# The same kernel under another recorded order of its tasks: two transformer layers with recurrent memory on one core

## The chip, the cores and the metric

One core of a Trainium2 chip runs the whole program. The time is in device microseconds, from the first to the last instruction and what lies around them; the median of the runs counts. A profiled execution has a span of its own, which is a little shorter than its time.

## The reference

Four stages run one after another on x (2048 tokens of 512 numbers): memory attention, gated FFN, memory attention, gated FFN, each on the layernorm of x and added to x. The two attention stages use the same weights, and so do the two FFNs.

```
def _A_ref(x, mem0, Wq, Wk, Wv, Wo, seg_len):      # H = 32 heads of 128, M = 8, seg_len = 32
    mem = mem0
    for s in range(n_seg):                         # 64 segments
        xs = x[:, s * seg_len:(s + 1) * seg_len, :]
        h = jnp.concatenate([mem, xs], axis=1)     # 40 rows
        q, k, v = h @ Wq, h @ Wk, h @ Wv           # per head (einsum)
        p = softmax(where(mask, q @ k.T * scale, -1e9))
        o = (p @ v) @ Wo                           # summed over the heads
        mem = o[:, :M, :]
        outs.append(o[:, M:, :])
    return concatenate(outs)

def _B_ref(x, w_gate, w_up, w_down):               # F = 1792
    return (sigmoid(x @ w_gate) * (x @ w_up)) @ w_down

x = x + _A_ref(layernorm(x), ...); x = x + _B_ref(layernorm(x), ...)
x = x + _A_ref(layernorm(x), ...); x = x + _B_ref(layernorm(x), ...)
```

The memory makes the segments a chain: a segment's first 8 rows of output are the next segment's memory.

## The kernel before

The kernel runs the two attention stages interleaved. A step (`emit_step`, line 876) takes segment t of the first layer and segment t - 6 of the second one together, so that a product has 80 columns (40 rows of each); there are 70 steps, 58 of them with both layers. In a step the 32 heads go in groups of six (one of two): products for q and k of three heads (line 953), the scores (988), mask, softmax on DVE and ACT (1002 to 1019), a transpose of P by TensorE (1033, three heads together as 128 columns), a spreading of P (1040 to 1047), P times V (1062), and the product with Wo (1080), which adds up all heads in one PSUM bank. After four segments an FFN block runs (`ffn`, 1135), whose weights stream in through GpSimd's queue (POOL).

V is made apart from that. The x rows of V don't depend on the memory, so `v_pass` (732) makes them for 128 rows at a time in eight blocks of 512 columns (742): a block's PSUM bank is copied into a staging tile, and a transfer stores it in a scratch array in DRAM (`scr`). The steps load their rows from there (921). The memory rows of V are made within a step (`strips`, 867) and go by transfers from SBUF to SBUF (933). The start of the kernel makes many V passes beforehand, while the weights still land: passes with `boot` stage two blocks together in the tiles of the FFN weights (`bootp`), and their stores go through SP or POOL, whichever the planner finds free. `v_half` (769) makes half passes. Before any V product, x tiles are loaded (829, 844), normalised (`layernorm_T`, 682) and transposed by TensorE (702); `load_mem0` (664) transposes the first memory (675).

Nothing is issued in the order of the code. Every piece of work is a task that `Planner.add` (243) takes with its engines, its duration, what it reads and writes, and the buffers that it uses. `Planner.plan` gives every task a rank from a long recorded string (`SEQUENCE`, line 61: a permutation of the 13,975 tasks), and `forward` (305) plays through them with the recorded durations: an engine that is free takes the task with the best rank among those that are ready and whose buffers are free. What comes out is the order on each engine, which engine does a copy that ACT or DVE could do, and which buffer each task gets. `lat` is the time that the planner reckons from a task's end until its readers may run; a reader of a stored V block is planned by the store's `lat`.

`warm` (450) looks for planned gaps over 250 ns on TensorE, and `run` (1284) fills them with matmuls on a tile of zeros (line 1306) ahead of the task behind the gap. These are ordinary instructions of the program: 123 of them, 54,912 columns in all.

```
for k, q in enumerate(unpack(SEQUENCE, len(T))):
    T[q].tail = -float(k)
order = self.forward()
```

In the built program SP first issues two chunks of Wv, six tiles of x and two more chunks of Wv; mem0 comes as the fourteenth. TensorE begins with 36 fillers, a layernorm transpose, 5 fillers, a transpose, 2 fillers, a transpose, two V blocks and the transposes of mem0.

Of the kernel before, what the change touches and what calls it, by code (L numbers as in the profile page):

```python
# [20 lines left out]
P = 128  # L21
MEM = 8
SEG = 32
L = MEM + SEG
# [12 lines left out]
def mm_ns(n):  # L37
    return max(n / 2.4 + 2.5, 25.0)
# [23 lines left out]
;B756%3T07011TGtd}$tIX)_K?aoXMjK$e5vW-dZtal;JHk{mI&QgWrBP)D^s=qIMTulb6#Ttex8Kf#~kv<HpT50CBI-Wv_<q6M!((->U-jq&7OXGm^aKUz-b1T~IwfdQy+_5vgcj*=+W!DBzdRHorO{Dd_S?ytV  # L62
X@7rCk^wxcAc)4=C`W%eB7ph_RA0xEwgUD}Il2H4j=NEEulF>SC>v4tcBxTgs^XsEp||WMAxE4XG}4z4h{P#HriIz5@sgq3p(``|;%O{6n9DN&9w@GGf?b)4gqABL7Mqk9J4weWwCX<#g8gt;=n4fzFl?OT7b2wp
p}=YmBVMk|m_ezF7HBVJgMCuiBDemSwzRvJ(+BJu^W`JnXdoZ|kmZn9#z_o#s~WV33xdfAt9G|T8V*OhQyX?Uz;x;->E>P1`f}sQk0-3NRRf{h8>N0+jEl$!))6nCL~2Gjwoh~l+c&{=ux~QXxRU8QLzHm)5V&UF
^BvX>gX?a!Y+aN6KL))kLfWZTB1>|NA3M1R*p)P#*obLmB4jW&8Lm}UnO(pg7yocsBrUHD1T`khRq{_oAuirMSfMfwg5-3DA&drFdO&*lK7|~j`q8Q9ehoO8+=RbpwJDGrkF><F+@9DxSxxkyL>Wg@z}vmg#|dcp
9h_y&7uDJixd;LTL%N>RG6IlV2at9doK%w7qqU#N-lom3D7jt%<n%j_ahIsI`zmF^QFN;ha)U&K-$Yf}k;D!O$?X3(8|wh%qwho@H<1i*``u5MYCS`_6XF2MEposi3H$mI7Djl$;{}FG0(O_|w}0usw!t-Q$Kx<c
YQ^$YZzlxQyA0&1XYIlO^|;Fi#L0Bq+CTGPI?Yl!dvj*CT}^+8M71Oep{!lmu@=}*YS%MvO!JppJoS4W;go^Sjm(3>RkqLCftth|_jd+ATMRX8qG!&_MNFEkfn$<Qh|oFR_YiL*@n1RS-Z!?iym$42_~Q3?U?M5Z
1|m@WYnrc(_(Tg@%3T(QT{3~u=C55b<J#XbY+sm9j5QT~s<@CJ4w2~7%Cy{)LY2(Ns$d+|=X-=^UIMYMw;%5qRrPUu>D-N&&oremdbeLUkiOQmDU4!3U)jxu=ee7U|6T3h1Y2#$^vvd(XNnfMLH#@FT{>BMD3q+1
13cJ{`AIV>6SWna>`{uSOqvUqNRB|5^kKTOu&Bj3U!-kabDd_CuNb=+m{Ha6IpeJR-cQX}Fok{JYBOhh+ND)dX*NE$u$Xxfn&ZQH=4CFY60MTs2@CjsIt4K%E5mQJM4$+Vv^iETZ(^toahRM-+%3zew`Vfy+xXcC
=B^YXWBj)RD|K&dT7u?~SuD0_QYeR8WfrkQPti6k!~=ekT_7x%&Rk=rl=3A^TC9dQgt<5Nqk{B4pDlG$r-C140<!iYq10n!l9^U%5VDWv(9Q6L^oEOew8I1DGVCO+9ijD7|6vfRe-rN>%4AahcsE>(VZoH$D_aiq  # L70
UdFEj2nhiX^~=pCqMCq(R+c&$>o=;=$u`h_0Wq0x{O<70OOQjN6Se6q064$r%qo|uw12gCQsC?1umzgIKYL#~-ooQU03i+8;TBBM3Ncb_7A%0Q@9pb8>`8p8#J)b4<Yo{s2wHj&fFF0>>s?eU@c!=z;IhJN><MY4
dm_q}5+t3d3zqz9!Vhk$Ey}C(bE0K<^m%dn;dqb>etDy8CuW4qDBZ3Qp+iF+1!wkhP#lWcIl;^(XfM&iym)!wuZ{TVkM(A?u{3N4tM~ZeY*clT?9&f4ZZ&Xm<4yRlK;`WPYI}}MWb^<;uqs-kx>c7@tkMh2^jNA1
i1K(7xyZ8N0!9h47ikR6@5g%0H=s74#SYl(o56>%^M-`e<XohImgJWHnaW=t7W@3Cq81oc?!@=gzAW24{{lOh#F-;3bV0MadMuG-83~<sd6+pNE>~k^TmD3&2t3%rx$l&<d(|41?&z87MH{U&07s6K)O?4}Go5{G
#cP1w05yW3-A|q3OGSd*Jr4<|+^`@5B?AgT%^YS2((mAe-9#3ya}xI~9*6v*t`3Gr+q{<Y(*0H*FJY!Fh3Bur38a7#5wOBdW+Aa9v<J=-3F};Hw5F#ay$IqA5?yrf6Yy_^m;_ba4lK>HUO*`VKAVIdvj6`rcyQ)(
J2aQeC**Z(pkHlUO5-XB`(pPJx_mQz&l-Qov(Z>#H*!&DYAHr)GG}4N0nG-mK-2B>MHIapk%U*n;3*WyB!fMNwR~zpLtD~X*H)KviKe@lRenrbzNc{<+Y#TpDkr?=B+i)90ozo;du~g|hc#rkL6I}yHvPnI=ef){
GjOx#bmBXj=rMKD>BUrXXi=rs9sYFj(WrJDEQ$)B<d~cp;6fD#ZTXSh{&r}QvBMTAQ!nXfpEF!qV9f+7@^!R`nYFoPe{64^8IY$UWoR>`6zg`(`8wu{(Mj^4sKQC4`u^p}1pf*d4;QKuGN|3%{uG~8XA@C#GK#TK
|MNCI$Rg?<y(g)5Iug<AChsqZWL&40hy84US%XF#P0O;+Y`I!A`&mi?PO-(~lPQZCd7Y<XM1gnB+91a}{iwf2Aq6QHsb)izB0Y}byOIV_!K2AY$nxjPw&z;p<u(m;Lag})0Lys17bQ4+Z1BlLY{uWx#h6}?s-8<v
isqPSpfY2MMgoBY`$Hd@`4dP5langGki~+qs0b|DiNAH^K(tyZ=N62Fd|i28RYODmVvV<2>?_E!lt`1bnk&(PxZ7p!p4P{CC$QQbTMZ~B!f6Ej%-mk<4a6}Ak4fe(X`DT6bFY-=-bPQx&R(A8o~h&wW=LAbDzx^C
*2S67IF&Ex8QuX4pa+6UO!`LA<-<j!1rQpC;)rrT>$d!}7m_y3zt?FN8B%@Op{)0P#V_c>c{rb6%Cc+KrkE~gJ426|C3rbyIs!y5KtzN#vu69BA^}6YOWJpIK~%*ilp=L8Ym4PxY;`d+7jGm`L#6o=C|kSRKxp+s
12q#}B9C0lT4PZr!!3Mi|BK<#3Nl~x!ub0u)V+mlINC)@&%B1k$0I1Z?v_7yNRmlxHq*e;Q%iT0+g{R#-6#$Li$s^h>~P@Ffx!Q`k+(nl(nyRxP1ll##izuCdVkgGU)QEW0w}pC-@k2ZpCLRWdZ$qo<eDLb9cDAP  # L80
3!qGZ#lcymlMU|F^0|ggOc`jev<hWTv_H+z%%y(3ezrAC)Cluy>pG>W-KKLeSzi84VHi$HR}dvnIAi-Yfxw=PFk9D#|Cn$%G?Lli=o!)35`VY%J2g~@qDFmrujR6*;k0-+K=>_7EXj=*13#G-Tno(3GRj@ZFf;E^
)MStRA1kyWf*z})0Q0GUnI*R)Re)aFhdRd=!6=o@TI3WnAPptA0y5<OXt_f;*qeOn`bCD=^B&nq|Nq@8+N>aO{Y-r=GjKi)z0(rlj+5$**8LycFjN}GbvSf4nboGRr*oM@KFd=XGave-nt+lQNU7XUxQ9;9JD?GT
K`IsG<=4^#j7{mwd3$P?ux_W`Nq5ZTv_k#Oyw@$8n@%$H{Qt)hbFY0UK62=LerA~X;x!wGWy>D5iVc*wgWCsTt#xx{O&aJh^%=WUW~Y$a0;!^AdOJ3C8MN}6G#=}fUwJ6Il-%gMmR6LGSeUz?Y`EN^Oa@Q;uE+Ie
Kbkh(Y{p>W5BTj^oSqWg{K0)2P<9@mb*T3lD7b4zj%e9zi!*Bbpn0gIA685bppYu;m9-)*Cc^1JXyjw@`*|*36VGc5`^eA~OLXT(oR)K3A&(Z>IJ$jih7p&CubfDeaS1vSk*Ez~ZH9ODh6{h*-CMq!Sv6%HiMko+
<2Jyw<0zq<rwD@wL*ZR5S37mG)xF`SV6;uBVyQ`Ax@MFofhBVm0%%V{gDbs#ZRa!<Exes`29q)JlbJ!kM}TPHAkD#`RDAR#Ss3LFjq7yRe*{{X{-3OFa+?FXQ1H7%lqNLzGmRBlyz$kn+7C%<jtG7Fm<)g@|1iDq
^q)*nuQ`vDOg**bB&GFNqmk%Q8$})k13+Q>;sK`<=>-K?dm^NGb-voa_UoyY0e~Y&)D4@X^U&-d0y|RjqJE;X^FlS3wOst}_ntnQlfomib-*cLDnRvBkAoMid9*;k*ciCRD7U*ts*vgDHcWv~fABk<8=gu3fFT|b
{)DPOllg)4_;wu#R$vG$zs*#|9)$r4@-yXAHk)lqZ`#n4=&jo0Gs0OUi9x|PAyd|I)Y`OdcpcBW&yC5=y>|%1f3{4sgGAp+oE_kwTJ4BR=!AqA_Pfs-p7jUkIpV=%;J|bQtZ??SLWiZw6SI^O>fGH-gD6RT$pfqF
Z<6|is?Azbab$@G@7Ln=i8DaY{oTXAF*#7Qt6T~LtZ^u?EL9fQzPT|gl(WPkOCY2gKSs}Ved5z~TmQ?@pe_#IgZRr7hwG`cW6=WL(-Q?>2>JT$Y?banab$d!)xa7cTA)UPKc_h-?sku5!}SiS?D=rE&y$_`-s!EI
KC8IvcD?VGQ-4HSo75G({ZlxJmLZc7p|ySPq!(*u*-_VfrKaj(&T31}QD9~tF16O8a5w+4gkBkx<-nk}Y_IyVHo>Db2>w1{?)Q77h@rt=H>s@nC9#UDN#pfnZrQ--m22UtEj(~W!G8;QHsDuPB`6f?tod4oMo5-@
KRu<Olb)8-agn3Df#xtD(c2?D6J;1)Xy`&1`*ervi0*&eSYTQ!nk}JqG1jZ{axYS>fbe&C_h?=W?nawC<jUMwX_7Zy(r+=qlWm3@4Zw858T_wE=qLx$)-Jo&5p(po>fb7dNWy6xultjBq~p8*g`Qo1c{c_;_;1)S  # L90
n3jg-*HA?tG6PYwY}H<ZxF0s8hg{t&S)3;oaQ4@q90@RdTr?sO;udDHG$el4uW_VaDr)|06SOzvZ9$F%i&(x4`j1bT6sR%Z0Oi6ieMV;cmJc+7S|HE-t#XopGR={##V}&qWw9<`+(e#*u&VkWV>lIizR<cVO;q%5
ZS;Kg02(So7Cb;7z$FQdkfJ%}PiWuQuf0YvgJ5@aC`s<oqOZaDuhv)DNdVnI5e7)93ZTiHpHMwtx;A`y2x4WsiGXmP9d|!{_=vDfY|W4aUfcIgb_0V9+=jS!rtld92)*dy+IW=QADwfHSaA8MR!=2F(w$SpxGv#y
nFfjtw_;W{Tm;Rg05uhRMc=U!FlJaj=U%IAdbQW<zjSpi-WObAFDl{}l8?)2Y_d(k{u0#uQ$(vVn#eo{fo}AJQ?v;pvO^c8=<%qoj>)n#Mnm<i>8B2~X$xSi+v?C-vP2s3KS)a(NFudF<IMM(4kWhSTvtVDf*h}|
bTx>%ckueI?)M>$%OjuT{{VhIit*9My`gkr_0G<PJ%UJ6WhTpfyy1$`9Ox^+1?UOllYTZw@~Au|0=tYL?UB4`eK3}?Rs@vOv0||2B9*{QT1`Kk;jH$&(}+1|ua?cmu^8uMxL@oBqd1uhe#7XPx;f>NV)3W*xo*a`
s{EyzGY$f)ddVUJozvMCf*3?1je}$4w9%2Xu)B-XvAB&0rrD9O?T(DnSl@O#{%IHd?Wp5>EfwC8N$>PDNuz)Fc_^?(|KiH{^5n(rJ}Io4FgJ?Sv$)R3gmn_?syKoG8;*B#tX|@0tqD|QF4VuvAtAvDUezf32AHg+
a^`&DC6uG)WzKv%Ej|h(GEtd!dU#wS@$e-Uk^RX(a8-li<<6#<Jj<l4A1A;>)w{u`%wJMw^YmW<6>RULEZbMq^MQ|TmCuLO#?kZU)vs(!LS#s;n-WRbXm~d&kJG%?F7i83$OO5(lcIZeE-9b6a~?$yogjr#>1Xgr
GY>c3@wEx~WqJ#rO3kyONoAPvvm@dxg0FASj~Pl&vbkIM*FsI8E6>8@DRExc(%bKXyX+&g<(|YrEq7EP#UyX_h0XtHonqXe<o?Z?{7?!jx4U>a!oteG2*YZV@Z(*5f@;S1+rJa)4(Y3y%$PQEvDWWcDJDJth?IMP
vmP4c#NK$!{Hms>f=J8q^xxg+S-F<aTQz!BwzvJga@^2kG8T2?v~YINX{KUF(T%$$1z8yev=DrQcQ%N~QO%HXNmcHb3mMq=(SrlO%RT8DvOz4kznxN*%+^r)9fr;7WeZDrb1UOKKJrI)BIvExOo$81upoQ##Hzs0
Bg(5c0z&I{z7_!)0zSp0v1~1*?Wy%KjrNm*x|o3$>>v`WJm%?5$>7dIF9ge(yfqJ5eCA+xmo7p%nSZ;`v3+56PS~PL`4^0_?evmI4pJW3a>uhrcXkO#JpS;Oned_RPX#2u3>XmqMN4!Fo>?*P0_z(DHe=JEj0!5P
x`q!3mNPKGg7nD5_2ozUD$=lu95n}G<1B~f_0eR!of5_-SztT~CHCo6PJglym@xtJrYQ{m*m$QF4UI7AetPvO29CFM6#X{!RIAPvcHO{U%Ddb)Dj4M_*WQ4&Si%v|Ls>Sv5lz(*^wPP^5J?w8H?`Uwxdy6?pK+**  # L100
nOq)NIV0@!IqktP8R_T?=5v(}F|&!s0$n}&K7tfc)q~e=+H@Ye#xfR;yvd255@Sl*M5-GT0;;=0BNDuiIp&w8mjyK`VJ8Gv#C-uff<en&3aIj{c<YzXJS!GXvA^w0Q>ciR5Xr4DtQVxPnC(iDI^Z`7;BB3xZ(<6M
mck?rQ~R{xRu~ITyIi*IzJW$03lk{DL5HvEjN$7}J?|DvpK&H4WIn~IDoGG(CUjw_MAwtJCkHq)nFSfMnXzcSEX{ryU?Q%^J{{sg|2yolB;~oNt*rwUv$iv*?ZfTTBQ_m-3cb@&z$HNqPEdSorx4UbEQCg@W|IHj
^$JdW({`|Ix+}pZ<jp1M+joYWW8<H`5lZB<*#en<_hXoqHbXd#E0L$;YT)G1j5giiOn8!bTc_Hd%JF7G5E)GqXG<`%v)N}hJWumP?;Pd)#-fHhApq>|T)0TzF$D*gvo(M_d|f(si2qbFN63qfrTENy&_C%La!Z^e
A3GI4jhp#~G&Wr#*6j8sjxF?1$5w%8ga1(tcT>?hIoU;Bd&dF9d?IM)y~AtbV~7L(IA)w~;=O+4{|}F#qs=bRuky@$LMe!4&jn4WooMIlB^T;RgqOZgY7<m9>H2e9A^NN#r>{7^^3K%$4aBOp!XTw`>Jh33+X_=x
# [1281 lines left out]
```

## Time and profile before

| what | us |
|---|---|
| median of 3 runs | 1788.54 (1787.59 to 1789.13) |
| the profiled execution, its time | 1789.13 |
| its span | 1787.1 |
| TensorE busy | 1765.1 (99%) |
| ScalarE (ACT) busy | 1201.9 (67%) |
| VectorE (DVE) busy | 1184.6 (66%) |
| GpSimd (POOL) busy | 579.0 (32%) |
| products for q and k, line 953 (two groups) | 614.7 and 615.0 |
| products with Wo, line 1080 | 356.2 |

TensorE's instructions overlap one another, so that a group's mean of one times its count is more than its busy time. The fillers count as busy. By stretches of the span, TensorE is idle for 1.9 us between 300 and 400 us, for 0.2 to 1.3 us in each 100 us from 400 to 1700 us, and for 6.1 us in the last 38 us. DMA moves 153 GB/s on the mean and 345 to 391 GB/s between 10 and 50 us, while weights, x and the stores of V pass at the same time.

### The profile page before, as it was taken

The numbers are of one execution on the slowest core, as the hardware profiler recorded it, in microseconds if no ns is written. First come the engines' busy times: TensorE is split into PE (matmuls) and PEld (weight loads), VectorE is DVE, ScalarE is ACT, GpSimd is POOL, SyncE is SP. The second block draws the span as 40 slices with busy tenths as digits, with TensorE's granted clock in tenths as the row PEclk, the third lists the DMA queues.
The fourth block names the chain that finished last, engine by engine and source line by source line (L and its number), as shares of the span: only waits on it lengthen the run. The fifth ranks groups of instructions, "written<-read, shape, count | busy, mean of one in ns | idle before, by whom it ended". The sixth has DMA issues, their size and how long they took to land.

```text
span 1787.1 us, 91201 instructions
## 1 busy us (share of the span) xinstructions
PE 1765.1 (99%) x39305; PEld 1505.1 (84%) x39305; DVE 1184.6 (66%) x4075; ACT 1201.9 (67%) x3244; POOL 579.0 (32%) x837
## 2 busy tenths in 40 slices
PE   9999999999999999999999999999999999999998
PEld 4578788888888888988898898888888888989886
DVE  3477666676577667766676677667766765667675
ACT  5677777676666667666676677667666766666564
POOL 5414032522333242323334241333325232333432
PEclk9999999999999999999999999999999999999999
DMA  9835255634555464546546453556546454554543
GB/s 350 274 87 163 77 163 138 201 108 117 165 161 152 127 192 122 160 115 174 154 136 184 136 163 107 145 161 169 153 127 198 117 146 122 162 154 139 161 139 97
DMA packets 144766, 273.37 MB, mean 153 GB/s; under 512 B 34306, under 2 KB 82314, under 8 KB 144362
## 3 DMA queue, kind: packets, MB, share of 16 engines
q0 software_dynamic: 56704, 183.16, 35.2%
q1 hardware_dynamic: 87658, 84.38, 16.8%
q8 instruction: 308, 5.05, 1.2%
q14 instruction: 96, 0.79, 0.2%
HBM read 221.78 MB, written 27.07 MB: 139 GB/s over the span
## 4 chain that ended last, share of the span: by engine, by line
PE 90%; ACT 4%; DVE 3%; DMA 1%; issue 1%; SPq 1%; DVEq 0%; POOL 0%; ACTq 0%; POOLq 0%
PE bank L953 31%; PE bank L1080 16%; PE bank L1182 10%; PE bank L742 7%; PE bank L867 7%; PE bank L1205 5%; PE bank L988 4%; PE bank L1062 4%; PE bank L1033 2%; ACT pbt L1312 1%; PE bank L1306 1%; DVE st L1002 1%; PE bank L702 1%; ACT qku L1320 1%; PE bank L1150 1%
## 5 line engine op out<-in xcount | busy, mean ns | idle before, releaser
L953 PE MATMUL bank<-hT,wk_sb 128*128 128x80 bf16 (+3 forms) x8960 | 614.7, 198 | 1.1 <-issue 1.1
L953 PE MATMUL bank<-hT,wq_sb 128*128 128x80 bf16 (+3 forms) x8960 | 615.0, 198 | 0.7 <-issue 0.5
L1320 ACT CAST qku<-bank 128x480 bf16<-128x480 f32 (+4 forms) x770 | 379.7, 507 | 211.4 <-PE bank L953 173.4
L953 PEld LDWEIGHTS <-wq_sb 128*128 128x128 bf16 x8960 | 452.1, 99 | 23.9 <-issue 12.8
L953 PEld LDWEIGHTS <-wk_sb 128*128 128x128 bf16 x8960 | 446.9, 99 | 1.2 <-issue 1.2
L1002 DVE TENSOR_TENSOR st<-bank,cst 40x240 f32<-40x240 f32 (+3 forms) x768 | 278.6, 368 | 157.9 <-PE bank L988 147.2
L1080 PE MATMUL bank<-otsb,wo_sb 128*128 128x80 bf16 (+1 forms) x8960 | 356.2, 198 | 1.5 <-ACT otsb L1320 0.7
L1080 PEld LDWEIGHTS <-wo_sb 128*128 128x128 bf16 x8960 | 334.9, 99 | 15.5 <-issue 2.8
L1175 POOL DMA_DIRECT2D wu<-in_B_w_up_dram x217 | 164.0, 756 | 284.6 <-PE bank L1182 123.1
L1174 POOL DMA_DIRECT2D wg<-in_B_w_gate_dram x217 | 163.9, 756 | 263.1 <-PE bank L1182 138.7
L1320 ACT CAST otsb<-bank 128x480 bf16<-128x480 f32 (+3 forms) x420 | 198.1, 482 | 44.9 <-PE bank L1062 29.3
L1199 POOL DMA_DIRECT2D wd<-in_B_w_down_dram x217 | 153.7, 709 | 198.0 <-PE bank L1205 85.4
L1312 ACT ACTIVATE pbt<-bank,pbt 80x160 bf16<-80x160 bf16 (+4 forms) x488 | 181.6, 381 | 27.5 <-PE bank L1033 18.0
L1012 ACT ACTIVATE st<-st 80x240 f32<-80x240 f32 (+3 forms) x420 | 159.2, 382 | 31.0 <-DVE st L1009 28.4
L692 POOL TENSOR_TENSOR pbt<-pbt 128x1 f32<-128x1 f32 (+1 forms) x80 | 45.3, 568 | 391.3 <-DVE pbt L691 390.7
L1182 PE MATMUL bank<-xnT,wg 128*128 128x128 bf16 (+2 forms) x1784 | 171.5, 218 | 0.4 <-DVE st L1009 0.4
L1014 DVE TENSOR_REDUCE pbt<-st 80x6 f32<-80x240 f32 (+3 forms) x420 | 151.4, 363 | 29.9 <-ACT st L1012 27.3
L1182 PE MATMUL bank<-xnT,wu 128*128 128x128 bf16 (+2 forms) x1784 | 171.0, 218 | 0.0
L988 PE MATMUL bank<-qku 128*128 128x80 bf16 (+1 forms) x2240 | 163.1, 198 | 0.5 <-ACT qku L1320 0.2
L1009 DVE TENSOR_TENSOR st<-st,pbt 80x240 f32<-80x240 f32 (+3 forms) x420 | 154.5, 369 | 3.3
L1019 DVE TENSOR_TENSOR pbt<-st,pbt 80x240 bf16<-80x240 f32 (+3 forms) x420 | 153.8, 369 | 4.3
L1007 DVE TENSOR_REDUCE pbt<-st 80x6 f32<-80x240 f32 (+3 forms) x420 | 151.9, 363 | 4.2
(104 smaller groups left out, 2413.8 us busy)
## 6 DMA issues: line engine op xcount, KB each, us to landing
wg<-in_B_w_gate_dram POOLq DMA_DIRECT2D x220, 256.0 KB, 4.3
wu<-in_B_w_up_dram POOLq DMA_DIRECT2D x220, 256.0 KB, 4.3
wd<-in_B_w_down_dram POOLq DMA_DIRECT2D x220, 256.0 KB, 4.3
vsb<-scr SPq DMA_DIRECT2D x345, 48.0 KB
vsb<-sst SPq DMA_DIRECT2D x372, 32.0 KB
scr<-vst SPq DMA_DIRECT2D x112, 96.0 KB
vsb<-scr SPq DMA_DIRECT2D x230, 24.0 KB
wv_sb<-in_A_Wv_dram SPq DMA_DIRECT2D x8, 512.0 KB
```

The source lines that it names most:

```text
L953: nc.tensor.matmul(o_ap, lhsT=W[:, c, h * P:(h + 1) * P], rhs=mv(c), start=(c == 0), stop=(c == DC - 1))
L988: nc.tensor.matmul(s_all(SB)[:, w0 + i, :], lhsT=fview(qku[:, i, 0, 0:1], [(1, P)]), rhs=qku[:, i, 1, 0:ncol], start=True, stop=True)
L1002: pl.add("DVE", dve_ns(n, True), lambda gsz=gsz, hs=hs, st=st, SB=SB, pj_=pj_, npj_=npj_, mk=mk, idx=idx: nc.vector.tensor_tensor(out=st[p ...
L1009: pl.add("DVE", dve_ns(n), lambda gsz=gsz, hs=hs, st=st, mx=mx: nc.vector.tensor_tensor(out=st[pr, hs], in0=st[pr, hs], in1=mx[pr, hs].uns ...
L1012: pl.add("ACT", act_ns(n), lambda hs=hs, st=st: nc.scalar.activation(out=st[pr, hs], in_=st[pr, hs], func=ACTF.Exp, scale=self.scale), r=s ...
L1019: nc.vector.tensor_tensor(out=pb[pr, 0:gsz * L].rearrange("p (h k) -> p h k", k=L), in0=st[pr, hs], in1=rs[pr, 0:gsz].unsqueeze(2).to_broa ...
L1080: nc.tensor.matmul(WB[:, c * ncol:(c + 1) * ncol], lhsT=self.wo[:, h, c * P:(c + 1) * P], rhs=otsb[:, hl, 0:ncol], start=(h == 0 and c == ...
L1174: pl.add("POOL", 760, lambda wg=wg, fs=fs: nc.gpsimd.dma_start(out=wg[:], in_=self.wgv[:, :, fs]), r=[("wo", self.H - 1)], w=[gk] + bt, la ...
L1175: pl.add("POOL", 760, lambda wu=wu, fs=fs: nc.gpsimd.dma_start(out=wu[:], in_=self.wuv[:, :, fs]), r=[("wo", self.H - 1)], w=[uk] + bt, la ...
L1182: nc.tensor.matmul(gu[:, 2 * i + k, 0:n], lhsT=W[:, c, i * P:(i + 1) * P], rhs=xnT[:, c, rw], start=(c == 0), stop=(c == DC - 1))
L1312: nc.scalar.activation(out=dst, in_=src, func=ACTF.Copy, scale=by)
L1320: nc.scalar.copy(out=dst, in_=src)
```

## The change

Two things are edited. The recorded string is another one (147 lines of text instead of 108). And in the tasks of `v_pass` and `v_half` two details differ.

```
 SEQUENCE = r"""
...
 """
...
             if k % w == 0:
                 vs = pl.buf(self.bootp if boot else self.vstp)
             o = 512 * (k % w)
-            own = ("own", len(pl.bufs)) if k % w == 0 else own
-            pl.add("PE", DC * mm_ns(512), vmm, r=keys + [("wv", h) for h in range(4 * k, 4 * k + 4)] + [own] * (k % w), w=[B] + [own] * (k % w == 0), use=[vs])
+            pl.add("PE", DC * mm_ns(512), vmm, r=keys + [("wv", h) for h in range(4 * k, 4 * k + 4)], w=[B], use=[vs])
...
-                       lambda vs=vs, d=d, c0=c0, n=n: ("dma", d, vs[c0:c0 + BLK * n, 0:512 * w]), lat=3000.0 + 3000.0 * boot,
+                       lambda vs=vs, d=d, c0=c0, n=n: ("dma", d, vs[c0:c0 + BLK * n, 0:512 * w]), lat=3000.0 + 2000.0 * boot,
...
-                           lambda lo=lo, i=i, dd=dd, flat=flat: ("dma", dd, flat()[64 * i + lo:64 * i + lo + 32, :]), lat=3000.0 + 3000.0 * boot,
+                           lambda lo=lo, i=i, dd=dd, flat=flat: ("dma", dd, flat()[64 * i + lo:64 * i + lo + 32, :]), lat=3000.0 + 2000.0 * boot,
```

Without `own`, the two V blocks that share a staging tile in a `boot` pass may come in either order on TensorE; with it the first one came first. And the planner reckons 5000 ns instead of 6000 ns from the end of a `boot` store's issue until its readers may run. Both act on the order alone; no instruction's work depends on them.

The change was announced as "the P transposes of three heads take 128 columns of weights, 8 of them unused, instead of 120; P tiles and small columns share one tile; same order". The line that sets `m = P if w == 3 else w * L` (1030) and the tile `pbt` that holds P tiles and small columns (558) are in both kernels, so that the edits above are all.

What the other string makes of the order, by a comparison of the two built programs, task by task:

| engine | tasks | at another place | of these beyond the engine's first 115 | most places |
|---|---|---|---|---|
| TensorE | 4202 | 574 | 471 | 34 at the start, 21 later |
| ACT | 3243 | 2644 | 2542 | 38, 13 |
| DVE | 4073 | 3335 | 3236 | 21, 11 |
| POOL | 826 | 159 | 81 | 23, 7 |
| SP | 1631 | 793 | 704 | 29, 18 |

75 copies go from ACT to DVE and 74 the other way; six stores change between SP and POOL each way, and both programs have 7 `boot` stores on SP and 57 on POOL. TensorE's products are the same ones. The fillers are 129 with 57,984 columns.

At the start SP now issues two chunks of Wv, mem0, three heads of Wq (0.39 MB), four tiles of x, two chunks of Wv, and so on; the last two of Wv's eight chunks are behind 7.88 and 8.60 MB of issued transfers, with their own bytes, where they were behind 7.09 and 7.81 MB. Among SP's eight issues ahead of the second step's five loads of V (line 921) four are now stores of V, and a fifth stands between these loads, where there was one. TensorE begins with 18 fillers, the transposes of mem0, 26 fillers, and four layernorm transposes with 1, 2 and 2 fillers between them; then come V blocks.

## The prediction

> **What bounds the kernel now.** I read the page first: the busy shares and the chain that ended last.
>
> ```profile
> PE 1765.1 (99%) x39305; PEld 1505.1 (84%) x39305; DVE 1184.6 (66%) x4075; ACT 1201.9 (67%) x3244; POOL 579.0 (32%) x837
> PE 90%; ACT 4%; DVE 3%; DMA 1%; issue 1%; SPq 1%; DVEq 0%; POOL 0%; ACTq 0%; POOLq 0%
> ```
>
> TensorE (PE) is busy for 1765.1 of 1787.1 us and holds 90% of the chain. DVE and ACT stand idle for a third of the span, so moving their work costs something only where PE is made to wait. A change that leaves PE's products alone can move the time only through PE's idle time and through its filler: line 1306 issues matmuls on a zero tile whose results nobody reads, where the planner foresees a gap. I therefore looked next at the start of PE's order of time.
>
> ```profile
> 1.00 9.97 PE L1306 MATMUL bank<-otsb 128*128 128x512 bf16 x36 [1.00 <-DVE otsb L606]
> 10.81 0.39 PE L702 MATMUL bank<-cst,xn 128*128 128x128 bf16 x4
> 11.03 1.08 PE L1306 MATMUL bank<-otsb 128*128 128x512 bf16 x5
> 11.95 0.39 PE L702 MATMUL bank<-cst,xn 128*128 128x128 bf16 x4
> 12.17 0.43 PE L1306 MATMUL bank<-otsb 128*128 128x512 bf16 x2
> 12.45 0.39 PE L702 MATMUL bank<-cst,xn 128*128 128x128 bf16 x4
> 12.87 1.90 PE L742 MATMUL bank<-wv_sb,xvf 128*128 128x512 bf16 x8
> 14.70 0.25 PE L675 MATMUL bank<-cst,hff 8*128 8x8 bf16 x4
> 14.89 1.47 PE L742 MATMUL bank<-wv_sb,xvf 128*128 128x512 bf16 x6
> ...
> 17.70 1.02 PE L742 MATMUL bank<-wv_sb,xvf 128*128 128x512 bf16 x4 [0.69 <-DVE xvf L1322]
> ```
>
> Columns: start, us, instruction, and in brackets the idle time before it with what ended it. The first useful product is at 10.81; nearly all of PE's free time before that is filler and shows as busy. Then the same engine by stretches (busy us and count of each engine, granted clock, DMA share, GB/s):
>
> ```profile
> 0.00:10.00 10.00, 9.00 (x32) 3.70 (x33) 3.59 (x15) 1.28 (x1) 7.18 (x29) 1.00 0.84 272
> 10.00:20.00 10.00, 9.27 (x65) 4.87 (x64) 6.05 (x25) 4.91 (x13) 5.68 (x10) 1.00 1.09 345
> 20.00:30.00 10.00, 10.00 (x61) 4.60 (x59) 4.47 (x18) 7.42 (x18) 6.51 (x12) 1.00 1.08 379
> ```
>
> The DMA engines are full (share above 1) from 10 us on, so in the first 30 us a transfer lands by the bytes queued ahead of it. From 300 us on PE is busy for 98.1 to 99.8 us of each 100, so there is little left to win or to disturb there.
>
> **The change, part by part.** As built, both programs hold the same products, evictions and transfers. What differs is their order on each engine, and the filler: 123 matmuls with 54,912 columns before, 129 with 57,984 after, so +3,072 columns. The words about transposes with 128 columns instead of 120 describe nothing that changes: the line that sets m to 128 for a group of three heads, and the shared tile of P and small columns, stand in both.
>
> *Price of filler.* Five matmuls with 2,176 columns go from 11.03 to the next start at 11.95: 0.92 us, 0.423 ns a column. The first 36, with 18,176 columns, take 9.81 us (1.00 to 10.81) where this price gives 7.69; the 2.12 us on top are a slow first stretch. [...]
>
> *A, the first 15 us.* In the new order PE runs 18 fillers (9,088 columns), the four small transposes of mem0 (line 675), 26 fillers (13,312), and then four layernorm transposes with 1 + 2 + 2 fillers (1,792) between them, before the first V product. The 18 fillers end at about 1.00 + 2.12 + 9,088 x 0.423 = 6.96. The mem0 transfer is moved up to third place on SP, behind 1.05 MB of Wv; the first x tile before, behind 1.18 MB, is first read at 6.74 (the row of DVE below), so mem0 lands just before 6.96. Then 0.19 for mem0 (14.70 to 14.89), 26 fillers 5.63: first layernorm transpose at 12.78; four of them 0.88, fillers 0.76: first V product at 14.42. Before, PE has by 14.89 done three transposes, mem0 and two V blocks (12.87 to 14.70, 1.83); taking those V blocks off and adding the fourth transpose gives 13.28. The new start is 1.14 us behind. Against that stands the 1.0 us that PE loses before to waiting on the xvf copies (0.69 is in the rows above). If the new order waits as much, A is +1.14; if not at all, +0.1. I take the middle, +0.6.
> What hides the x tiles (DVE's first reading, and for C the second step's V loads on SP):
>
> ```profile
> 6.74 0.69 DVE L689 BATCH_NORM_STATS2 pbt<-xs 128x6 f32<-128x512 bf16 x1 [5.09 <-DMA xs<-in_A_x_dram]
> ```
>
> ```profile
> 81.43 1.91 SPq L921 DMA_DIRECT2D vsb<-scr  x5
> ```
>
> SP now issues 0.39 MB of Wq ahead of them. First tile: 1.58 MB instead of 1.18 MB, at 345 GB/s 1.2 us later, about 7.9; from first bn_stats to first transpose is 4.07 us (6.74 to 10.81), so 12.0, under 12.78. Fourth tile: 1.97 MB, 9.0, needed by 14.2 - 4.07 = 10.1. Both covered, by 0.8 and 1.1 us; beyond that each us is a us of PE.
>
> *B, the last chunks of Wv.* Before, the last is behind 7.81 MB of issued transfers, now 8.60 MB: with 2.72 MB in the first 10 us and 3.45 in the next, it lands at 20 + 2.43 / 0.379 = 26.4 instead of 24.3. PE reaches the product that needs it (twelve V blocks of 0.865, four transposes of 0.22, one half pass of 1.85 and two more V blocks after 14.42) at 29.3. Covered by 2.9 us: 0. At 345 GB/s and with the 2.5 us of the shortest boot store on top it would be 29.5, so at most +0.3.
>
> *C, the stores of V while the kernel starts.* The planner now reckons 5.0 us instead of 6.0 behind the issue (some 0.55 us). The row:
>
> ```profile
> DMA to landing us min/median/max: 2.5/5.3/7.1
> ```
>
> The median fits both, the longest neither. Four of these stores now stand on SP among the eight issues ahead of the second step's five V loads, and a fifth between them (one before). If SP waits there, those loads, an x load, a save of kx and the second step's strip loads (92.72 on before) are queued behind it, and PE's PV products wait for the strip loads without cover. But the V loads are issued at 81.43 to 83.3, over 9 us earlier: a landing of 7.1 costs nothing. The bound is one weight tile of 256 KB (0.7 us at 350 GB/s) pushed into the strip loads: 0 to +0.7, I take 0. [...]
>
> *D, the rest.* 471 of the 4,087 later PE stages change place, mostly by one; 149 copies change between ACT and DVE; 704 SP issues move. The filler there is 128 columns less (-0.05). PE's named waits on V loads are two, and the chain in order of time passes through a transfer four times:
>
> ```profile
> PE bank L1062 <- DMA vsb<-scr: 0.6, 1, 0.6
> PE bank L1062 <- DMA vsb<-sst: 0.4, 1, 0.4
> ```
>
> ```profile
> 218.98 3.06 DMA kx<-xq
> 312.58 4.17 DMA vsb<-sst
> 497.36 3.41 DMA vsb<-scr
> 1347.98 2.95 DMA vsb<-scr
> ```
>
> With 0.5 us a wait: four new ones +2.0, both old ones gone -1.0; I take +0.5. The last 38 us (31.93 busy) keep their order of products but for a few weights of the FFN: 0.
>
> Sum: 0.6 + 0 + 0 + 0.5 - 0.05 = +1.05 us on the profiled 1787.1, so a span of 1788.2. That execution took 1789.13; the median of the runs is 1788.54, so the forecast is 1789.6. Bounds: 0.1 - 1.0 - 0.05 = -0.95 and 1.14 + 0.3 + 0.7 + 2.0 - 0.05 = +4.1.
>
> **The rivals.** *Slower: the start's transfers set PE's pace.* If the queues share bandwidth among what is issued instead of serving in order, the two Wv chunks issued right behind the x tiles (1.05 MB) come with them: the fourth tile lands at 6.74 + (3.02 - 1.18) / 0.345 = 12.1, its transpose is at 16.1 instead of 14.2, and the filler has run out. +1.9 on A's 1.14, with C's 0.7 and D: +4.2, so 1792.7. It decides from a landing after 10.1. For it: DMA share 1.09. Against: by 6.74 some 1.6 MB can have moved before (2.72 MB of the first 10 us less 3.26 us at 345 GB/s) and 2.9 MB had been issued, so the first tile didn't share with all of it.
> *Faster side: the new start doesn't wait for xvf and D's two waits go.* -0.95: 1787.6. Against it: the gain is bounded by rows that add up to 2 us, and 1.3 us more filler is certain.
> *Nothing at all:* the words' transposes are unchanged, so the time is 1788.5; it speaks against this that the order did change.
>
> **How the numbers follow.** A measurement of this kernel can tell about 0.2%, 3.6 us, from no change: 1785.0 to 1792.1. Forecast (with the nothing case) 0.62, slower rival 0.27, faster side 0.11. Of the forecast 0.03 lies above 1792.1; of the slower rival 0.02 below; of the faster side 0.06 beyond -0.2%. So faster 0.06, same 0.66, slower 0.28. The range takes both bounds, the slower rival and a spread like that of the runs shown (0.8): 1787.0 to 1794.0.
>
> **What would show it.** The first V product at 14 to 15 us (right), after 16 (the slower rival); the product of the last Wv chunk without idle time before it; PE's wait on V loads at most 3 us in all; filler 129; the stretches from 300 us on as before within 0.5 us each. Wrong would be: a new wait in the steady steps that comes back every step, since 58 steps with both layers at 0.5 us are 29 us.

## The result, and the profile after

The changed kernel takes 1797.64 us (median of 20 runs, 1794.94 to 1803.75), the kernel before 1788.57 (20 runs on the same chip, 1786.39 to 1793.41). The ratio is 1.0051, 95% interval 1.0042 to 1.0060: 9.1 us slower, where 1.1 us (1787.0 to 1794.0 in all) had been forecast. The profiled execution took 1800.80 us with a span of 1798.9, 11.8 us more than before. A profiled execution can be one of the longest of its kernel: this one is 3.2 us above the median, those of e1, e2, e5, e9 and e14 below are 4.6 to 7.4 us above theirs, and what is read in such a profile is more than the median run's.

The page of the changed kernel, its busy time and the chain that ended last:

```profile
PE 1765.5 (98%) x39311; PEld 1504.5 (84%) x39311; DVE 1189.3 (66%) x4076; ACT 1197.1 (67%) x3243; POOL 578.8 (32%) x837
...
PE 87%; ACT 4%; SPq 2%; DMA 2%; DVE 1%; issue 1%; POOL 0%; DVEq 0%; ACTq 0%; POOLq 0%
```

PE is busy for 0.4 us more than before, so the other 11.4 us are idle time of PE. The same engine by stretches, changed kernel (columns as in the prediction):

```profile
10.00:20.00 10.00, 8.54 (x56) 4.38 (x55) 6.95 (x28) 5.88 (x15) 3.63 (x7) 1.00 1.10 347
...
40.00:50.00 10.00, 8.90 (x90) 4.76 (x89) 2.17 (x6) 8.18 (x19) 5.51 (x11) 1.00 1.06 371
50.00:60.00 10.00, 6.28 (x74) 3.42 (x73) 2.23 (x8) 3.78 (x9) 3.97 (x8) 1.00 1.05 382
```

Before, these stretches held 9.27, 10.00 and 10.00 us of PE; the last two:

```profile
40.00:50.00 10.00, 10.00 (x125) 5.66 (x126) 3.47 (x11) 6.93 (x16) 5.45 (x11) 1.00 1.05 391
50.00:60.00 10.00, 10.00 (x109) 4.96 (x108) 0.00 (x0) 6.75 (x13) 4.57 (x9) 1.00 0.99 349
```

A little over half of the loss, 6.3 us, is in three waits of the start (1.46, 1.10 and 3.73 us). Comparing when each kernel starts the same piece of PE's work (at places where both have done the same set of pieces), the changed kernel is 5.8 us behind at 83.8 us of the kernel before, 5.0 at 150, 6.0 at 500, 9.8 at 1300 and 12.3 at 1780: one part lost in the start, the other a little at a time.

*First wait, the start of PE's order of time:*

```profile
13.30 0.43 PE L1343 MATMUL bank<-otsb 128*128 128x512 bf16 x2
15.19 0.40 PE L740 MATMUL bank<-cst,xn 128*128 128x128 bf16 x4 [1.46 <-DVE xn L731]
15.47 3.63 PE L780 MATMUL bank<-wv_sb,xvf 128*128 128x512 bf16 x16
```

The fourth layernorm transpose waits 1.46 us for DVE. DVE and ACT at that time, changed kernel:

```profile
14.61 0.19 DVE L1359 COPY hT<-bank 128x56 bf16<-128x56 bf16 x1 [1.60 <-ACT xvf L1357]
14.72 0.41 DVE L731 TENSOR_SCALAR xn<-xs,pbt 128x512 bf16<-128x512 bf16 x1
```

```profile
12.59 1.28 ACT L1357 ACT_TABLE_LOAD   x1 [12.59 <-PE bank L740]
13.88 0.31 ACT L1357 COPY hT<-bank 128x56 bf16<-128x56 bf16 x2
14.08 0.88 ACT L1357 COPY xvf<-bank 128x384 bf16<-128x384 bf16 x2
```

DVE's layernorm stands behind a copy of hT that waits for ACT's xvf copies, and these stand behind ACT's load of its function table. In the kernel before that load ran at 0.74 us:

```profile
0.74 1.28 ACT L1320 ACT_TABLE_LOAD   x1 [0.74 <-PEq L1367]
```

It stands ahead of ACT's first copy in both kernels. By the traces the old first copy (xvf, at 11.23 us) waits for PE alone, and that wait stands on the copy; the new one (hT) waits for PE and for GpSimd, whose memsets of hT run from 4.89 us, and of these two waits the one for PE stands ahead of the load, until 12.59 us.

*Second and third wait, ACT and then PE, changed kernel:*

```profile
40.57 0.58 ACT L1357 CAST wg<-bank 128x512 bf16<-128x512 f32 x1 [5.57 <-DMA scr<-wg]
...
49.73 0.59 ACT L1357 CAST wu<-bank 128x512 bf16<-128x512 f32 x1 [0.32 <-DMA scr<-wd]
55.27 0.58 ACT L1357 CAST wd<-bank 128x512 bf16<-128x512 f32 x1 [4.96 <-DMA scr<-wg]
...
56.35 0.47 ACT L1357 COPY xvf<-bank 128x128 bf16<-128x128 bf16 x1
```

```profile
41.21 1.02 PE L780 MATMUL bank<-wv_sb,xvf 128*128 128x512 bf16 x4 [1.10 <-ACT wg L1357]
...
52.12 1.03 PE L780 MATMUL bank<-wv_sb,xvf 128*128 128x512 bf16 x4
56.88 2.76 PE L780 MATMUL bank<-wv_sb,xvf 128*128 128x512 bf16 x12 [3.73 <-ACT xvf L1357]
```

Two copies of V blocks into a boot staging tile stop ACT for 5.57 and 4.96 us until a store of that tile's former content has landed. The bracket of the second names a store of wg, but the copy waits for several; by the trace the last of them to land was a store of wd that SP had issued,

```profile
43.52 0.71 SPq L1353 DMA_DIRECT2D scr<-wd  x1
```

and that landed at 55.17, 11.7 us after its issue. For the first it was GpSimd's store of wg, issued at 34.08 and landed at 40.47. Behind the second stands an xvf copy that the next V product needs. Matched with the plan, both copies belong to the second of two V blocks that share a tile (k odd), and in both cases that block runs ahead of the first (k even). The planner hands the tile out when the first block starts (`T[bf.users[0]].acq`, the first in the order of the code), so a second block that goes first writes a tile that still belongs to somebody else, and the plan knows of no wait: it sets the two copies at 35.45 and 49.32 us, ahead of its own time for the landing of the tile's former stores (46.02 and 57.97). The rule `own` that the change takes out of v_pass kept that from happening: no pair is reversed before, sixteen are in the new order.

*The steady steps*: PE's waits on the loads of V (`vsb<-scr`) and of the memory rows' strips (`vsb<-sst`) after 170 us (total, times, longest), and transfers in the chain that ended last, changed kernel:

```profile
PE bank L1099 <- DMA vsb<-sst: 4.4, 5, 1.7
...
PE bank L1099 <- DMA vsb<-scr: 1.7, 2, 0.9
```

```profile
551.07 3.76 DMA vsb<-sst
...
945.70 5.77 DMA vsb<-scr
951.49 3.17 DMA vsb<-scr
961.40 5.05 DMA vsb<-sst
```

Seven waits with 6.1 us, where before there were two with 1.0. Not every late load shows under its name: from 170 to 1750 us PE stands idle ahead of the PV products (P times V, line 1062 before, 1099 now) for 2.2 us before and for 11.3 now, by all causes that the profile names, and ahead of everything else for 6.3 and 5.0. So what is lost behind the start is lost ahead of the PV products.

### The profile page after: what moved, and what is told of

Read it like the earlier page. It is cut to its first block, busy times and chain, and to the rows that moved or that the text cites. A ratio compares the mean times of both kernels' runs of the same rounds, so it can differ in the third digit from the quotient of the medians.

```text
span 1798.9 us, 91186 instructions
## 1 busy us (share of the span) xinstructions
PE 1765.5 (98%) x39311; PEld 1504.5 (84%) x39311; DVE 1189.3 (66%) x4076; ACT 1197.1 (67%) x3243; POOL 578.8 (32%) x837
## 4 chain that ended last, share of the span: by engine, by line
PE 87%; ACT 4%; SPq 2%; DMA 2%; DVE 1%; issue 1%; POOL 0%; DVEq 0%; ACTq 0%; POOLq 0%
PE bank L990 31%; PE bank L1117 16%; PE bank L1219 9%; PE bank L904 7%; PE bank L780 6%; PE bank L1242 5%; PE bank L1099 4%; PE bank L1025 4%; SPq L970 2%; PE bank L1070 2%; ACT pbt L1349 2%; DMA vsb<-sst 1%; DMA vsb<-scr 1%; PE bank L740 1%; PE bank L1343 1%
## 5 line engine op out<-in xcount | busy, mean ns | idle before, releaser
L1357 ACT CAST qku<-bank 128x480 bf16<-128x480 f32 (+3 forms) x770 | 380.4, 507 | 209.9 <-PE bank L990 177.3
L1349 ACT ACTIVATE pbt<-bank,pbt 80x160 bf16<-80x160 bf16 (+5 forms) x477 | 177.7, 381 | 29.0 <-PE bank L1070 19.9
```

What stands on the lines that cost most here:

```text
L1349: nc.scalar.activation(out=dst, in_=src, func=ACTF.Copy, scale=by)
L1357: nc.scalar.copy(out=dst, in_=src)
```

## The experiments

Ratios are to the kernel before on the same chip (its median there was 1789.2 to 1791.8 us), five rounds each. The last columns say how far PE is behind the one profile of before (span 1787.1) at 150 and at 1780 us of it, worked out from the starts of PE's weight loads; since the kernel before was itself 0.7 to 3.3 us longer in these series than in the first (1788.57), about that much of the last column is not the edit's. Where the profiled execution was a long one (see above), that shows in these two columns too.

| | start (to 155 us) | rest | ratio (95%) | at 150 | at 1780 |
|---|---|---|---|---|---|
| changed | new | new | 1.0051 (1.0042 to 1.0060) | 5.0 | 12.3 |
| e1 | new, two copies mended | new | 1.0025 (1.0013 to 1.0036) | 1.7 | 15.6 |
| e2 | new, table early | new | 1.0059 (1.0040 to 1.0079) | 12.9 | 18.5 |
| e5 | new, both | new | 1.0018 (1.0003 to 1.0034) | 1.2 | 11.1 |
| e3 | new | old | 1.0062 (1.0040 to 1.0084) | 7.7 | 8.4 |
| e4 | old | new | 1.0026 (1.0011 to 1.0041) | 1.1 | 9.2 |
| e13 | new, both | old | 1.0009 (0.9998 to 1.0020) | 1.9 | 4.9 |
| e8 | old, both changed lines | old | 1.0041 (1.0024 to 1.0059) | 4.4 | 6.8 |
| e10 | old, rule out | old | 1.0035 (1.0017 to 1.0052) | 3.2 | 8.7 |
| e11 | old, latency | old | 1.0020 (1.0005 to 1.0035) | 2.0 | 6.4 |
| e12 | new, rule back | new | 1.0087 (1.0064 to 1.0111) | 10.7 | 22.1 |
| e6 | old | new, SP old | 1.0004 (0.9993 to 1.0014) | 1.4 | 3.3 |
| e7 | old | old, SP new | 1.0023 (1.0013 to 1.0033) | 0.5 | 8.2 |
| e9 | new, both | new, SP old | 1.0020 (1.0004 to 1.0036) | 2.4 | 15.2 |
| e14 | new | new, SP old | 1.0063 (1.0046 to 1.0080) | 8.2 | 19.1 |
| e15 | old | old, stores off SP | 0.9994 (0.9984 to 1.0004) | 1.1 | 2.7 |
| e16 | new | new, stores off SP | 1.0028 (1.0017 to 1.0039) | 7.1 | 7.2 |
| e17 | new, both | new, stores off SP | 0.9997 (0.9984 to 1.0010) | 2.9 | 3.8 |

### The two faults of the start

e1, in the changed kernel's plan(), the stores that the two copies have to wait for:

```diff
         T = self.tasks
+        for i, ds in ((152, (127, 128)), (195, (252, 253, 254, 255)),):
+            T[i].deps.update(ds)
```

> The changed kernel with two dependences more: the copies of two second-half V blocks (the one that ran at 40.57 us and the one at 55.27 us) stand behind the boot stores of the tile that they write. Only ACT's and DVE's orders and four places of PE move. Theory: without the rule that the removed line set, a second half can run before its first half, while the tile still belongs to the V blocks before; its copy then waits for their stores, which the plan doesn't know, and what stands behind it on ACT (an xvf copy) holds PE. PE's idle time of 1.27 us at 39.1 and of 3.73 us at 56.9 should go, some 0.5 us may come back because the PSUM banks stay taken: -4.5 us against the changed kernel, about 1793.1 us, ratio 1.0026 to the kernel before. Rival: the V products stand still for as long anyway, because the stores' landing holds their PSUM banks: no change, 1797.6 us, ratio 1.0051.

Measured: 1.0025, where 1.0026 was expected. The windows of the same stretch, and ACT and DVE there:

```profile
50.00:60.00 10.00, 9.89 (x130) 5.96 (x131) 3.31 (x11) 6.73 (x16) 3.64 (x7) 1.00 1.02 367
```

```profile
51.27 0.44 ACT L1359 COPY xvf<-bank 128x128 bf16<-128x128 bf16 x1
```

```profile
57.66 0.69 DVE L1361 CAST wd<-bank 128x512 bf16<-128x512 f32 x1 [0.99 <-DMA scr<-wu]
```

The plan now gives both copies to DVE; the second, which has to wait for the stores, runs there at 57.66. The xvf copy on ACT no longer stands behind it (51.27 in place of 56.35), and PE has 9.89 us in place of 6.28. At 83.8 us the kernel is 1.6 us behind in place of 5.8. SP and GpSimd issue the same transfers in the same order; what has moved is what stood behind the wait. The rival (banks held as long) falls.

e2, an ACT instruction in setup_consts:

```diff
         nc.vector.memset(self.negh, -0.5)
+        nc.scalar.copy(out=self.th[0][:, 0, 0:1], in_=self.negh)
```

> The changed kernel with one more ScalarE copy of 128x1 in the set-up, ahead of everything. Theory: ACT's first copy waits for two engines in the new order, so one of the waits stands on the load of the function table (1.28 us at 12.59), which in the kernel before was done at 0.74. With an earlier ACT instruction the load goes to the first two microseconds; the first xvf copies, DVE's copy behind them and the fourth layernorm transpose come 1.0 to 1.3 us earlier: about 1796.4 us, ratio 1.0044. Rival: the fourth layernorm is late for its x tile, and PE waits for that instead: no change, 1797.6 us.

ACT and PE at the start of e2:

```profile
0.74 1.28 ACT L646 ACT_TABLE_LOAD   x1 [0.74 <-PEq L1405]
```

```profile
14.18 0.40 PE L741 MATMUL bank<-cst,xn 128*128 128x128 bf16 x4 [0.17 <-DVE xn L732]
14.45 3.63 PE L781 MATMUL bank<-wv_sb,xvf 128*128 128x512 bf16 x15
```

In the place itself the theory holds: the wait is 0.17 in place of 1.46, and the first V product starts at 14.45 in place of 15.47. The time shows nothing of it (1.0059). With the two copies unmended PE reached their wait earlier, and in the profiled execution it lasted 5.58 us; the clock granted to PE then fell to 0.50, for 6.8 us in all. e2 in windows of 2 us (length, busy and count of PE, granted clock, DMA share, GB/s):

```profile
54.00:56.00 2.00, 0.00 (x0) 0.89 1.00 369
56.00:58.00 2.00, 0.00 (x0) 0.50 1.01 360
58.00:60.00 2.00, 1.17 (x3) 0.50 0.97 338
60.00:62.00 2.00, 2.00 (x6) 0.50 0.98 345
```

The 12 matmuls of 512 columns behind the wait take 4.34 us (58.83 to the next start at 63.17); at the fillers' 0.423 ns a column it would be 2.60. Besides, PE now waited 2.0 us for the last Wv chunks.

e5, both edits together:

> The changed kernel with both edits of the start: the two copies behind the stores of their tile, and the early ScalarE copy that loads the function table. Theory: the two account for the loss of the start, so that at the 115th piece of PE's order (83.8 us before) the kernel stands 0.3 to 0.6 us behind the kernel before (5.8 in the changed kernel, 1.6 with the two copies alone), and up to 2 us more if the last Wv chunks are late for the earlier products, as they were with the early table alone. With the new steady order behind it: ratio 1.0020 to 1.0028. Rival: the start stays at +1.6 or more because the table's 1.0 us only turns into a wait for Wv: 1.0025 to 1.0032.

1.0018. Its profile is 1.8 us behind at 83.8, more than the 0.3 to 0.6 expected; but the same 18 fillers at the start took 6.80 us in it and 5.38 in the changed kernel's profile, 1.42 us that have nothing to do with the edits. Less these it is 0.4. That the table's 1.0 us shows in the time too isn't shown: e5's interval overlaps that of e1 (1.0025), which has the two copies alone.

### Which of the changed lines

e8 has both changed lines with the old recorded order, e10 the rule alone, e11 the latency alone; e12 is the changed kernel with the rule put back. The two edits:

```diff
-            own = ("own", len(pl.bufs)) if k % w == 0 else own
-            pl.add("PE", DC * mm_ns(512), vmm, r=keys + [("wv", h) for h in range(4 * k, 4 * k + 4)] + [own] * (k % w), w=[B] + [own] * (k % w == 0), use=[vs])
+            pl.add("PE", DC * mm_ns(512), vmm, r=keys + [("wv", h) for h in range(4 * k, 4 * k + 4)], w=[B], use=[vs])
```

```diff
-                       lambda vs=vs, d=d, c0=c0, n=n: ("dma", d, vs[c0:c0 + BLK * n, 0:512 * w]), lat=3000.0 + 3000.0 * boot,
+                       lambda vs=vs, d=d, c0=c0, n=n: ("dma", d, vs[c0:c0 + BLK * n, 0:512 * w]), lat=3000.0 + 2000.0 * boot,
```

(the second in v_half too).

> The kernel before with the changed lines alone (the rule of first half before second half taken out, the boot stores' latency 2 us instead of 3 behind the base) and its own recorded order. Without the rule nine second halves run ahead of their first halves, and one copy is planned about 3.8 us before the stores of its tile can have landed (6 us from their issue). Theory: ACT stands still for some 4 us there, and PE loses 1 to 4 us in the first 90 us, nothing later: ratio 1.0005 to 1.0022. Rival: the lines cost nothing without the new order: 1.0000.

> The kernel before with its own order, the rule of first half before second half taken out, the stores' latency as before. Theory (the rule is what matters of the lines): the same copy is planned 3.8 us before the stores of its tile can have landed, ACT stands still there, and the time is that of both lines together: 1.0025 to 1.0050. Rival (the latency matters): 1.0000 to 1.0010.

> The kernel before with its own order and the boot stores' latency of 2 us instead of 3 behind the base alone. It moves 17 places on PE, 43 on ACT, none on SP and POOL, and adds 5 filler matmuls. Theory: 1.0000 to 1.0008. Rival (the latency matters): 1.0025 to 1.0050.

> The changed kernel with the rule of first half before second half back, with the new recorded order. No second half runs first, 145 places on PE move, and 33 more filler matmuls stand in gaps that the plan now sees (at most 33 x 512 columns x 0.423 ns = 7.1 us). Theory: PE's idle time behind the xvf copy and behind the copy into wg goes (5.0 us of the changed kernel), but the order was recorded without the rule, so PE waits for tiles by plan instead, as filler: 1.0035 to 1.0070 in all, no gain that can be told from the changed kernel's 1.0051. Rival: the rule alone mends the start: 1.0020 to 1.0030.

e8, ACT at the copy that was named beforehand, and PE:

```profile
33.88 0.59 ACT L1319 CAST wd<-bank 128x512 bf16<-128x512 f32 x1 [0.27 <-DMA scr<-wu]
40.30 0.59 ACT L1319 CAST wu<-bank 128x512 bf16<-128x512 f32 x1 [5.83 <-DMA scr<-wu]
```

```profile
40.94 1.89 PE L742 MATMUL bank<-wv_sb,xvf 128*128 128x512 bf16 x8 [1.43 <-ACT wu L1319]
```

So the wait comes with the lines, not with the new string: 1.0041, more than the 1.0022 expected. e10 shows the same stop (6.2 us on ACT) and 1.0035. e11 has no ACT wait on a store above 0.3 us and is 0.5 us ahead at 84 us; its 1.0020 lies between the two expectations, and what it loses it loses later, so the latency's part isn't settled, but the stop is the rule's. Putting the rule back into the new order (e12) is no cure: 1.0087, beyond even the upper end of 1.0070. That order was recorded for tiles without the rule; with it PE is 10 us behind at 95 us, and the program has 162 fillers with 73,984 columns, 16,000 more than the changed kernel's, 6.8 us at 0.423 ns a column.

### Start and rest apart

Only the recorded string differs (`new` and `old` are the tasks in the order in which each plan starts them):

```
e3:  first = [q for q in new if start_new[q] < 155e3];  SEQUENCE = first + [q for q in old if q not in first]
e4:  first = [q for q in old if start_old[q] < 155e3];  SEQUENCE = first + [q for q in new if q not in first]
e13: as e3, with the two edits of the start
```

> The changed kernel with another order: the new order for all tasks that it plans in the first 155 us, the old order for all others. Theory: the time is lost in two places, 5.8 us in the first 90 us and the rest (3.3 us of the medians) in new waits of the steady steps that come from the new order itself: 1788.6 + 5.9 = 1794.5 us, ratio 1.0033. Rival A, the start alone, which shifts the transfers of the steady steps against PE and so makes the later waits too: 1797.6 us, ratio 1.0051. Rival B, the steady order alone, the start being absorbed later: 1788.6 us.

> The kernel before with another order: the old order for all tasks that it plans in the first 155 us, the new order for all others. Theory: the new order's steady steps alone cost 3.3 us: 1791.9 us, ratio 1.0018. Rival A (start alone): 1788.6 us, ratio 1.0000. Rival B (steady order alone): 1797.6 us, ratio 1.0051.

> Both cures of the start, and the whole rest (after 155 us of the plan) in the old order: against the run with SP alone in the old order (1.0020, 1.0004 to 1.0036) only PE's, ACT's and DVE's orders of the rest differ. If SP's order is the whole of the rest's loss: about as that run, and both near 1.0010. If PE's, ACT's and DVE's new orders of the rest cost something on top: 1.0000 to 1.0008, below that run. If the start's cures themselves leave the steady steps worse off: 1.0020 again.

e4, 1.0026, shows that the new order loses in the steady steps behind an old start as well (1.0018 expected); it excludes that the start alone does it. e3 loses 0.7 us behind 150 us in its profile, so its loss is in the start. Its 1.0062 is above the 1.0033; in its profile the 18 fillers at the start took 6.61 us (5.38 in the changed kernel's), and a wait of 2.34 us was followed by 3.41 us at a granted clock of 0.50 (some 1.7 us lost, an estimate: half of them). Whether that makes up the difference of the medians isn't shown. e13, both cured and the old rest, has the lowest ratio of those with the new start and all stores on SP, 1.0009; its interval reaches those of e5 and e9, so it doesn't decide among the three cases that were expected.

### SP's queue

In e6, e7, e9 and e14 the issues on SP behind 155 us stand in the other kernel's order, each in one of the places that SP's issues have in the string:

```
sel = [k for k, q in enumerate(base) if on_SP[q] and start[q] >= 155e3]
for k, q in zip(sel, sorted((base[k] for k in sel), key=other.index)):  SEQUENCE[k] = q
```

> The old start and the new rest, with the issues on SP after 155 us in the old order (686 places on SP move, 7 on PE). Theory: the steady waits come from SP's order, in which a V load that waits for the store of its V stands ahead of strip loads: the waits on V and strip loads after 170 us fall to the level of the kernel before (about 1 us in all), PE's idle time at the pieces planned at 290, 690, 996, 1298 and 1502 us goes, ratio 1.0000 to 1.0010. Rival: PE's order asks for these loads earlier; then the waits stay, ratio 1.0020 to 1.0030.

> The kernel before with the issues on SP after 155 us in the new order (668 places on SP, 75 on PE, move). Theory (SP's order makes the waits): as the new rest with its own SP order, ratio 1.0015 to 1.0030, with PE waiting 4 us or more on V and strip loads. Rival (PE's order): 1.0000 to 1.0008, waits on these loads at most 2 us.

> The changed kernel with all three causes taken out: the two copies behind the stores of their tile, the early load of ACT's function table, and SP's issues after 155 us in the old order. Theory: start +0.4 us against the kernel before (5.8 less 4.3 for the copies and 1.0 for the table), rest +0.7 (1.0004 with the old SP order): 1.0002 to 1.0012. If one of the three only hid a fourth cause, the ratio stays at 1.0020 or more. Not below 1.0000, since the new start has 3,200 more columns of filler.

> The changed kernel with nothing but SP's issues after 155 us in the old order (686 places on SP, 7 on PE). If SP's order costs the 0.2% that it cost on the kernel before: 1.0051 - 0.0020 = 1.0031. If it costs nothing here: 1.0051.

The ratios of e6 (1.0004) and e7 (1.0023) came out as the theory of SP's order had it; e6's interval and e4's just overlap. In e6's profile PE's idle time ahead of PV products (170 to 1750 us) fell to 5.9 us from e4's 8.9, not to the 2.2 of before; the waits that the profile names after the loads are 1.8 us, where about 1 was expected. e7's largest named wait after 170 us:

```profile
PE bank L1054 <- DMA vsb<-sst: 4.1, 4, 2.0
```

e9 (1.0020) and e14 (1.0063) did not: with SP's old order behind the new start PE's idle time ahead of PV products was 10.8 and 11.5 us, at other steps. So the order on SP is not the whole of it. What all profiles have in common is that SP issues back to back ahead of a step's PV products: the issues of the ten strip loads take 0.59 us each (median), but behind 170 us in every profile, before's included, 64 to 77 of some 617 take 0.95 us or more, at other places each time. A load that is late by a microsecond would then hold PE wherever the order has less spare than that; this is the reading that e15 to e17 test, by taking work off the queue, in v_pass:

```diff
-                pl.add(("SP", "POOL") if boot else "SP", {"SP": 450, "POOL": 590} if boot else (430 if n == XS else 710),
+                pl.add(("SP", "POOL") if boot else "POOL", {"SP": 450, "POOL": 590} if boot else 590,
```

> The kernel before with all 224 later stores of V (96 and 32 KB) issued by GpSimd in place of SP. If the steady waits come from SP's queue, in which loads stand behind stores that are issued for 0.3 to 0.7 us each, SP gets some 110 us free and the waits on V and strip loads fall under 1 us: 0.9985 to 1.0000, faster than both kernels. Rival: GpSimd issues them late (it waits for PE before each weight load, up to 12 us) and they take 5 us to land in place of 3, so that V loads wait for them: 1.0030 or more.

> The changed kernel with its 224 later stores of V issued by GpSimd in place of SP (49 places of PE move). If the rest's loss comes through SP's queue: PE's waits on V and strip loads after 170 us fall from 6.1 us to 1 us, the start's loss stays, and of the 1.0051 some 1.0025 to 1.0038 are left. If the rest's loss has another way (PE's, ACT's or DVE's order itself): 1.0045 or more.

> Both cures of the start and the 224 later stores of V issued by GpSimd, with the new order throughout. If the loss is the two faults of the start and SP's queue: 0.9992 to 1.0010, about as the kernel before with the same stores moved (0.9994), less than its own 1.0018 with the stores on SP. If the new order of PE, ACT and DVE costs more of its own: 1.0015 or more.

PE's waits on these loads after 170 us in e15, and the only ones in e16:

```profile
PE bank L1054 <- DMA vsb<-sst: 0.7, 1, 0.7
PE bank L1054 <- DMA vsb<-scr: 0.6, 1, 0.6
```

```profile
PE bank L1053 <- DMA vsb<-sst: 1.2, 3, 0.7
```

e16 loses nothing behind 150 us (7.1 there, 7.2 at the end) with the new order throughout; its 1.0028 is the start's loss. e17 has both cures and the moved stores: 0.9997, no difference from the kernel before that can be told, nor from e15 (0.9994); against e5, the same without the moved stores, the intervals just overlap, and its profile still has two waits on strip loads, 2.8 us, one of them of 2.0. In the three profiles PE's idle time ahead of PV products is 2.8, 2.8 and 4.9 us. So the loss behind the start goes when the stores leave SP's queue, with the new order kept throughout and the start mended or not. What it is of the stores there that delays the loads isn't shown: they take SP's time for 224 issues (some 0.6 us each), and ahead of them SP waits for the copies that they read; both left the queue together. The rival of e15, stores that land late, is there in SP's waits in e15, and costs PE no more than the 1.3 us above:

```profile
SPq L913 <- DMA scr<-vst: 90.2, 43, 7.8
```

SP's loads wait 90 us in all for the stores (10.8 before), but SP has the time. e15 and e17 are faster than the changed kernel; that either beats the kernel before, as was expected of e15, is not shown. Open stays why SP's old order mended the rest behind the old start and not behind the new one.

## Why the prediction was wrong

*The reading of the change.* That products, evictions and transfers stay as they are, and that the words about 128 columns describe nothing that differs, held: PE is busy 0.4 us more, with 129 fillers.

*A, the first 15 us (+0.6, at most +1.14).* The transfers were sized well: first x tile read at 8.06 (forecast 7.9), no wait for a tile. The first V product came at 15.47 in place of 14.42. The missing term is the table load, 1.0 us of PE's time; without it, in e2, it came at 14.45.

*B, the last Wv chunks (0, at most +0.3).* PE didn't wait for them in the changed kernel, as forecast. But with the start mended it waited 2.0 to 2.1 us in e2, e9 and e17, and not at all in e5 and e13: the cover of 2.9 us was reckoned too wide, and what the changed kernel lost elsewhere may have hidden it.

*C, the boot stores (0, at most +0.7): the step that failed.* It asked what is queued behind the stores on SP. It did not ask which engine writes the tiles that the stores empty, and the removal of `own`, the one part of the change that takes an order away, got no price at all. What came in place of the 0: second blocks run ahead of first ones, ACT stands still for 5.57 and 4.96 us until the stores of the tile's former content have landed, and PE loses 1.10 + 3.73 us behind it. e1 took 4.2 us of that away, from 1.0051 to 1.0025. The row of landings that was read (2.5, 5.3, 7.1 us) covers the 57 stores that GpSimd issued, and not the seven on SP; these landed by the trace in 3.5 to 9.2 us before, and the two longest in the changed kernel took 10.9 and 11.7. So the bound of 7.1 us that C went by did not hold for SP's stores.

*D, the rest (+0.5, at most +2.0).* The mechanism, waits on these loads, was right and mis-sized: 6.5 us in the profiled execution from 83.8 us on, some 3.3 in the medians (9.1 less 5.8, if the start costs the median run as much as the profiled one). Each was priced at 0.5 us; the largest are 1.7 us in the changed kernel and 3.3 in e5. Of the signs named beforehand, at most 3 us of such waits came out at 6.1, and the stretches of 100 us from 300 us on left their 0.5 us (98.54 us busy from 700 to 800, 99.62 before).

*The clock.* The forecast has no term for it. In the changed kernel's profile a wait of 3.73 us came, and the granted clock stayed at 1.00; in e2 it fell to 0.50 in a wait of 5.58 us, and to 0.50 behind far shorter ones too, 2.07 us in e1 among them (last section).

*The rivals.* The slower one put the loss into landing x tiles; these were in time. "Slower" had 0.28, nearly all by that cause; the two faults of the start were in none of the cases.

## What to carry to other kernels

Where a change takes a dependence away, ask who writes the buffer that it guarded, and what stands behind that writer on its engine: an order that the planner may now choose can wait on the chip for something that the plan doesn't model (here ACT for 5.57 and 4.96 us, for stores to land). Look at the first instruction of ACT whenever its order changes; here an early ACT instruction (a copy of 128x1 in e2) put the table load at 0.74 us in place of 12.59. On SP, which issues without pause ahead of the bound engine, 64 to 77 of some 617 strip loads took 0.95 us or more to issue (median 0.59), at other places in each profile; here taking work off the queue took the loss away with the start mended or not, and another order on it only behind the old start.

## What the runs showed of the hardware

Of 19 idle times of PE of 2 us or more in all the profiles, 11 had a granted clock of 0.50 behind them or in their last part, the shortest of them 2.07 us (e1). It lasted 3.41 us (some 1.7 us lost where PE is busy in it, an estimate: half of them), and twice that in two cases, with 3.31 us (e5) and 5.58 us (e2). The other 8 had none, with 3.73 us (changed kernel), 3.12 us (e4), and 2.87 and 2.86 us (e1, e12) among them, while even 1.69 us in e2 and 1.98 us in e14 were followed by one. So in these profiles the length of one pause doesn't tell whether the granted clock falls behind it; what does isn't shown. In the steady steps the 2.07 us of e1 so cost some 3.8 us by this estimate, and 2.08 us in e12, with the clock at 1.00 behind them, no more than themselves.

The same 18 fillers at the start took 5.35 us (e14) to 6.80 us (e5) from one execution to the next, where their 9,088 columns at 0.423 ns make 3.84. What sets the difference isn't shown; up to 1.4 us of a time are settled before the first useful product.
